# Banded attention with a two-layer FFN: the softmax division of units 16 to 47 moves from VectorE to ScalarE, and the hand-written order of all engines is written anew

## The chip, the cores and the metric

One core of one Trainium2 chip runs the kernel. The metric is device microseconds of one execution, lower is better. Engine names are those of the profile: PE is TensorE, DVE is VectorE, ACT is ScalarE, POOL is GpSimd, and SP is SyncE, which issues most of the DMAs.

## The reference

Four sequences of 768 tokens, eight heads of 64. Each token attends to 8 global tokens and to the last 96 tokens, with a bias that grows with distance. The softmax is divided by its row sum, and the result goes through a two-layer FFN (512 to 2048 to 512) with a leaky ReLU.

```python
scores = scale * np.matmul(q, k.transpose(0, 1, 3, 2)) + bias
scores = np.where(keep, scores, -1000000000.0)
scores = scores - np.max(scores, axis=-1, keepdims=True)
a = np.exp(scores)
a = a / (np.sum(a, axis=-1, keepdims=True) + 1e-09)
attn = np.matmul(a, v)
h = x @ w_in                      # x: 3072 x 512, w_in: 512 x 2048
g = np.maximum(0.01 * h, h)
out = g @ w_out                   # w_out: 2048 x 512
```

## The kernel before

**Work and stages.** The 3072 tokens are 24 steps of 128 tokens, and each step is two *units* of four heads, 48 units in all. Attention runs unit by unit and feeds the FFN. The FFN works on chunks of 3, 3, 2 and then four times 4 steps. The first three chunks are multiplied in the plain way, 16 hidden blocks each (48 blocks, words `F0` to `F47` and `H0` to `H47`); from the fourth chunk on each pair of blocks is made from seven smaller products (`Q`), which need sums of weight blocks and of activations. Every factor is kept as a high and a low part, so that each product is three matmuls.

**Who sets the order.** A table `ORDER` of 2574 words is walked by `fast_path` from first to last. Each word issues the instructions of one small step, and nearly all are pinned to that order on their own engine. Engines wait for one another through semaphores, but each runs its own instructions strictly in the table's order: an instruction that waits holds up everything behind it on its engine. The same is true of the DMA issues on SP and on POOL.

**The words.** For unit n: `Lq Lk Lv` load (SP); `S` scores (PE, L319); `B` adds the bias and takes the row maximum (DVE, L336); `E` exponentials and row sums (ACT, L352); `N` adds a small constant and inverts the sum (DVE, L377 and L378). Up to unit 15 the division lies in a small diagonal matrix (`G`, POOL) by which PE transposes (`T`). From unit 16 (`BY_DVE`) on, `M` divides, one instruction for each of four heads (DVE, L389, in `divide`); `D` transposes on DVE (L394) and sends the tile to DRAM (SP, L363); `I` fetches it back, turned, in four DMAs (SP, L369). `V` multiplies by the values (PE, L473) and `Xh` copies the result out (ACT, L483). `M` has parts `.0` to `.3`, as `B` and `E` have.

For FFN block n: `F` makes the hidden block (PE, L1051 to L1053); `ga` copies it out (ACT, L1063), `gb` applies the leaky ReLU (DVE, L1065), `gc` rounds the high part (ACT, L1067), `gd` makes the low part (DVE, L1069); `H` multiplies by the second weights (PE, L1087 to L1089). `H` needs `gc` for its first matmul and `gd` for its third. `c0` to `c31` convert the weights at the start.

For the later chunks: `C` makes sums of weight blocks for eight pairs (POOL L675, with four rounding steps each on ACT, L678); the sums of the first six pairs are built in one scratch area, stored to DRAM by `b` (SP, L726), and loaded back into weight memory that is no longer needed by `e` (POOL's DMA queue, L732; two loads for each pair, 768 KB for part `.0` and 256 KB for part `.1`). A pair's sums can only be started when the store of the pair before has left the scratch area. `A`, `Y`, `z` make sums and high and low parts of the activations (POOL L736, ACT L739, DVE or POOL L742). Then `Q` (PE, L711), `d y r h l` (adding up, ReLU, high and low part: DVE L756 L760 L766, ACT L750 L763), `J` (PE, L774) and `R` (weights from DRAM, POOL's queue, L722).

```python
for word in ORDER.split():
    step(word)
```

In `step`, `M` calls `divide(n, part)`, `D` calls `turned(n)`, which calls `move`, and `I` calls `fetch(n)`; `late` holds `C b e A Y z Q d r h l J R`.

Of the kernel before, what the change touches and what calls it, by code (L numbers as in the profile page):

```python
# [11 lines left out]
F32 = mybir.dt.float32  # L12
# [34 lines left out]
T7 g1c c8b F2 K7 k7 c9a N8 Lw11 c8c g1d V7 G8 g2a c9b S9 Lv10 Xh7 Xl7 T8 Lq6 H1 B9 Lk12 c9c Lw12 K8 k8 g2b E9 c8d V8
c9d S10 Lv11 g2c N9 Xh8 F3 g2d G9 Lk13 c10a B10 c11a Xl8 E10 c10b T9 H2 g3a N10 K9 Lw13 g3b k9 G10 c10c c11b g3c V9
T10 Lv12 Xh9 c10d Lw14 c11c Xl9 S11 K10 g3d F4 c12a B11 Lq7 k10 Lk14 E11 c11d H3 c12b g4a c13a N11 Lw15 c12c g4b V10
G11 c13b g4c F5 Lv13 Xh10 Xl10 g4d Lw16 c13c c12d T11 g5a S12 c13d c14a H4 K11 g5b Lk15 k11 B12 g5c E12 g5d V11 c14b  # L50
c15a S13 Lv14 Xh11 F6 Xl11 N12 Lw17 c14c c15b G12 H5 g6a B13 Lw18 c15c E13 g6b c15d F7 c14d g6c c17a g6d c16a N13 c17b
T12 g7a H6 K12 G13 k12 g7b Lw20 c17c c16b g7c F8 P6.0 P6.1 g7d Lw19 P6.2 c17d c16c T13 g8a c16d H7 g8b c18a g8c c18b
c19a F9 g8d Lw21 c18c c19b H8 g9a g9b Lw22 c19c c18d g9c F10 g9d c20a c19d c20b c21a H9 g10a g10b Lw23 c20c c21b g10c
F11 g10d Lw24 c21c V12 c20d g11a c21d H10 c22a Lv15 K13 g11b k13 c22b g11c c23a F12 g11d Lw25 c22c c23b S14 g12a H11
g12b Lw26 c23c B14 g12c E14 g12d F13 c22d c23d c24a N14 c25a H12 c24b G14 g13a g13b Lw27 c24c F14 c25b g13c T14 g13d
Lw28 c25c c24d g14a H13 g14b c26a c25d g14c g14d c27a F15 c26b H14 c27b Lw29 c26c g15a g15b Lw30 c27c F16 c26d g15c
g15d c28a c27d H15 c28b g16a c29a g16b Lw31 c28c F17 c29b g16c Lk16 O0 g16d c29c c28d g17a H16 O1 g17b c30a c29d g17c
O2 g17d c31a F18 c30b O3 O4 H17 c31b c30c g18a O5 g18b c31c C0.0 O6 F19 c30d g18c C0.1 g18d O7 c31d C0.2 H18 g19a O8
C0.4 C0.3 g19b C0.5 g19c O9 g19d F20 C0.6 Lk17 C0.8 C0.7 O10 C0.10 C0.9 H19 g20a O11 C0.11 g20b g20c O12 C0.13 C0.12
g20d F21 C0.14 O13 C0.15 Lq8 H20 C1.0 g21a O14 g21b C1.1 g21c O15 C1.2 g21d F22 C1.4 b0 C1.3 C1.5 H21 g22a C1.6 Xh12  # L60
g22b Xl12 g22c C1.7 g22d V13 C1.8 S15 Lv16 Xh13 K14 C1.10 F23 k14 Lq9 B15 C1.9 Xl13 Lk18 E15 Z2 H22 g23a N15 g23b g23c
V14 P22.0 g23d G15 S16 P22.1 Lv17 P22.2 F24 C1.11 Lk19 B16.0 Xh14 B16.1 E16.0 C1.13 B16.2 B16.3 E16.1 E16.2 Xl14 T15
E16.3 g24a N16 H23 C1.14 C1.12 M16.0 K15 M16.1 k15 C1.15 M16.2 M16.3 C2.0 V15 D16 b1 S17 C2.1 g24b Xh15 F25 C2.2 B17.0
g24c B17.1 E17.0 B17.2 Lk20 C2.4 E17.1 B17.3 C2.3 g24d E17.2 C2.8 S18 E17.3 I16 g25a H24 C2.5 N17 C2.9 g25b C2.6 Lk21
M17.0 g25c M17.1 C2.10 Lq10 C2.7 F26 M17.2 Lv18 M17.3 C2.11 g25d C2.13 B18.0 C2.12 B18.1 H25 E18.0 B18.2 C2.14 E18.1
B18.3 E18.2 D17 C2.15 E18.3 g26a N18 V16 Xl15 g26b I17 F27 Xh16 M18.0 g26c M18.1 M18.2 M18.3 Lv19 g26d S19 b2 g27a D18
H26 g27b B19.0 g27c B19.1 E19.0 F28 g27d E19.1 Lq11 B19.2 B19.3 I18 E19.2 E19.3 V17 C3.0 g28a N19 S20 g28b Lk22 Xh17
C3.1 H27 Lv20 M19.0 g28c C3.2 B20.0 Lk23 B20.1 E20.0 B20.2 C3.4 E20.1 B20.3 E20.2 g28d F29 E20.3 C3.8 M19.1 C3.3 N20
# [96 lines left out]
def fast_path(ctx, tc, qp, kp, vp, wi, wo, nvec, weights, wiboth, woboth, nmall, out, B, H, S):  # L165
# [999 lines left out]
```

## Time and profile before

| | |
|---|---|
| median of 3 runs | 662.97 us (662.08 to 663.45) |
| the profiled execution | 663.38 us, of which the span from first to last instruction is 661.6 us |
| PE busy | 622.5 us (94% of the span), granted clock 0.992 of full |
| DVE busy | 490.9 us (74%) |
| ACT busy | 279.9 us (42%) |
| POOL busy | 197.7 us (30%) |
| DMA | 130.64 MB, 197 GB/s on average |

PE is in use for nearly the whole span, so what the time can still lose is what PE stands idle, and what it runs at less than full clock. The share of PE is an average over stages: the first units and weight conversions, the plain chunks, and from about 300 us on a long even stretch of `Q` and `J`. A view by stage says where PE stands idle, and the view of waits says for whom.

### The profile page before, as it was taken

The numbers are of one execution on the slowest core, as the hardware profiler recorded it, in microseconds if no ns is written. First come the engines' busy times: TensorE is split into PE (matmuls) and PEld (weight loads), VectorE is DVE, ScalarE is ACT, GpSimd is POOL, SyncE is SP. The second block draws the span as 40 slices with busy tenths as digits, with TensorE's granted clock in tenths as the row PEclk, the third lists the DMA queues.
The fourth block names the chain that finished last, engine by engine and source line by source line (L and its number), as shares of the span: only waits on it lengthen the run. The fifth ranks groups of instructions, "written<-read, shape, count | busy, mean of one in ns | idle before, by whom it ended". The sixth has DMA issues, their size and how long they took to land.

```text
span 661.6 us, 16121 instructions
## 1 busy us (share of the span) xinstructions
PE 622.5 (94%) x6188; PEld 534.9 (81%) x6188; DVE 490.9 (74%) x1277; ACT 279.9 (42%) x801; POOL 197.7 (30%) x277
## 2 busy tenths in 40 slices
PE   5589999999999987889999999999999999999996
PEld 4478888898778865778888888888888888889894
DVE  7999999965867668497777976777987846655543
ACT  5978767546644353442224333234433223211111
POOL 3433401168553378280003400014300015200000
PEclk9999999999999999799999999999999999999998
DMA  8866645794767869656667497677686542433331
GB/s 292 288 223 203 212 138 174 279 418 139 226 218 246 286 203 311 180 171 193 192 200 223 129 283 223 169 209 231 181 257 187 160 144 68 160 114 107 96 96 69
DMA packets 64197, 130.64 MB, mean 197 GB/s; under 512 B 9072, under 2 KB 27504, under 8 KB 63344
## 3 DMA queue, kind: packets, MB, share of 16 engines
q1 hardware_dynamic: 53744, 91.78, 43.0%
q0 software_dynamic: 10368, 37.75, 19.1%
q8 instruction: 51, 0.84, 0.6%
q14 instruction: 34, 0.28, 0.2%
HBM read 96.47 MB, written 33.03 MB: 196 GB/s over the span
## 4 chain that ended last, share of the span: by engine, by line
PE 72%; DMA 10%; DVE 8%; ACT 4%; issue 2%; SPq 2%; POOL 1%; DVEq 0%; ACTq 0%; POOLq 0%
PE ps_q L711 13%; PE ps_two L774 12%; PE ps_o L774 12%; PE ps_o L711 9%; DMA room<-via 4%; PE ps_av L473 4%; DMA via<-pr 3%; PE ps_av L319 3%; PE ps_h L1051 3%; PE ps_h L1053 3%; PE ps_h L1052 3%; PE ps_o L1087 3%; PE ps_o L1089 3%; PE ps_o L1088 2%; ACT pr L352 2%
## 5 line engine op out<-in xcount | busy, mean ns | idle before, releaser
L763 ACT CAST rounded<-room 128x512 fp32r<-128x512 f32 x64 | 39.7, 620 | 194.4 <-DVE room L760 188.3
L722 POOL DMA_DIRECT2D wo<-w x60 | 32.2, 536 | 272.6 <-PE ps_two L774 257.9
L774 PE MATMUL ps_two<-wo,rounded 128*128 128x512 f32 x320 | 95.2, 395 | 0.0
L774 PE MATMUL ps_o<-wo,rounded 128*128 128x512 f32 x320 | 94.8, 394 | 0.0
L352 ACT ACTIVATE pr<-pr,nmall 128x192 f32<-128x192 f32 (+1 forms) x192 | 83.9, 440 | 17.6 <-DVE nmall L336 17.2
L756 DVE TENSOR_TENSOR room<-ps_o,room 128x256 f32<-128x256 f32 x128 | 54.1, 423 | 39.2 <-PE ps_o L711 29.0
L756 DVE TENSOR_TENSOR room<-ps_q,room 128x256 f32<-128x256 f32 x96 | 40.1, 418 | 34.0 <-PE ps_q L711 33.4
L1051 PE MATMUL ps_h<-rounded,wi 128*128 128x384 f32 (+1 forms) x192 | 62.6, 326 | 1.2 <-ACT atz L1063 1.1
L1052 PE MATMUL ps_h<-rounded,wi 128*128 128x384 f32 (+1 forms) x192 | 61.0, 318 | 0.6 <-POOL rounded L497 0.6
L1053 PE MATMUL ps_h<-rounded,wi 128*128 128x384 f32 (+1 forms) x192 | 60.9, 317 | 0.0
L774 PEld LDWEIGHTS ps_two<-wo,rounded 128*128 128x128 f32 x320 | 54.0, 188 | 6.1
L711 PEld LDWEIGHTS ps_o<-rounded,wo 128*128 128x128 f32 x384 | 53.9, 188 | 5.9 <-DVE pr L394 0.3
L774 PEld LDWEIGHTS ps_o<-wo,rounded 128*128 128x128 f32 x320 | 53.6, 188 | 5.8
L336 DVE CUSTOM_DVE_ANT_0 pr<-ps_av,nbw 128x192 f32<-128x192 f32 x140 | 42.3, 352 | 19.1 <-ACT room L483 14.1
L711 PE MATMUL ps_o<-rounded,wo 128*128 128x256 f32 x384 | 56.1, 282 | 0.0
L711 PE MATMUL ps_q<-rounded,wi 128*128 128x256 f32 x384 | 55.3, 280 | 0.4 <-ACT room L750 0.4
L711 PEld LDWEIGHTS ps_q<-rounded,wi 128*128 128x128 f32 x384 | 51.8, 189 | 3.8 <-ACT room L750 0.7
L760 DVE SCALAR_TENSOR_TENSOR room<-room 128x512 f32<-128x512 f32 x64 | 48.1, 753 | 1.7
L473 PEld LDWEIGHTS ps_av<-room,vr 64*64 64x64 f32 x1472 | 31.4, 134 | 21.8 <-issue 11.4
L675 POOL TENSOR_TENSOR room<-room 128x256 f32<-128x256 f32 (+1 forms) x56 | 45.4, 821 | 8.2 <-ACT room L678 5.8
L473 PE MATMUL ps_av<-room,vr 64*64 64x64 f32 (+1 forms) x1472 | 37.8, 239 | 8.1 <-DMA room<-via 6.7
L389 DVE TENSOR_SCALAR pr<-pr,rs 128x192 f32<-128x192 f32 (+1 forms) x128 | 43.8, 381 | 0.6
(131 smaller groups left out, 1322.8 us busy)
## 6 DMA issues: line engine op xcount, KB each, us to landing
wo<-w POOLq DMA_DIRECT2D x60, 512.0 KB, 3.8
via<-pr SPq DMA_DIRECT2D x28, 384.0 KB, 3.9
room<-via SPq DMA_DIRECT2D x112, 96.0 KB, 4.1
kr<-in_kp_dram SPq DMA_DIRECT2D x40, 256.0 KB, 4.6
vr<-in_vp_dram SPq DMA_DIRECT2D x40, 256.0 KB, 3.8
room<-in_wo_dram SPq DMA_DIRECT2D x16, 512.0 KB, 4.7
room<-in_wi_dram SPq DMA_DIRECT2D x16, 512.0 KB, 4.4
w<-wo SPq DMA_DIRECT2D x16, 512.0 KB, 8.2
```

The lines of the kernel that those rows point to most:

```text
L336: pin(nc.vector.tensor_tensor_reduce(out=head(u, pr, a, j), in0=own(u, ps[:, j, a * KW:(a + 1) * KW]), in1=nb, scale=-0.125, scalar=3.0e38 ...
L352: pin(nc.scalar.activation(out=p, in_=p, func=AF.Exp, scale=-1.0, bias=nm[:, 2 * a + j:2 * a + j + 1], accum_out=sm[:, 2 * a + j:2 * a + j ...
L389: pin(nc.vector.tensor_scalar(out=p, in0=p, scalar1=rs[:, n:n + 1], scalar2=1.0, op0=ALU.mult, op1=ALU.mult))
L473: tc.keep_in_program_order(nc.tensor.matmul(av[out, a, cols], lhsT=v[rows, t, j, :], rhs=near(rows, j, t, f), start=n == 0, stop=n + 1 == ...
L675: pin(nc.gpsimd.tensor_tensor(out=out, in0=a, in1=b, op=op))
L711: tc.keep_in_program_order(nc.tensor.matmul(out, lhsT=lhs[:, k], rhs=rhs[:, k], start=k == 0 and m == 0, stop=k == 1 and m == 2))
L756: pin(nc.vector.tensor_tensor(out=quarter[i][o], in0=lps[b][:, h * HB:(h + 1) * HB], in1=quarter[a][q], op=ALU.add))
L760: pin(nc.vector.scalar_tensor_tensor(out=t, in0=t, scalar=0.01, in1=t, op0=ALU.mult, op1=ALU.max))
L774: tc.keep_in_program_order(nc.tensor.matmul(o, lhsT=lhs, rhs=rhs, start=f == 0 and m == 0, stop=f == NF - 1 and m == 2))
L1051: tc.keep_in_program_order(nc.tensor.matmul(ps, lhsT=wh, rhs=xh[:, k, :CT], start=(k == 0), stop=False))
L1052: tc.keep_in_program_order(nc.tensor.matmul(ps, lhsT=wh, rhs=xl[:, k, :CT], start=False, stop=False))
L1053: tc.keep_in_program_order(nc.tensor.matmul(ps, lhsT=wl, rhs=xh[:, k, :CT], start=False, stop=(k == NK - 1)))
```

## The change

Two edits. In `divide` the multiplication by the inverse row sum is an activation (copy with a scale for each partition) on ACT in place of a tensor-scalar on DVE, for all units from 16 on (32 units, four instructions each). And `ORDER` holds the same 2574 words in another order.

```diff
@@ ORDER (2574 words, the same ones in another order) @@
-k2 K2 G3 Lw5 B4 Xh1 c2c V2 Xl1 E4 c3b S6 Lv5 T3 Lk9 Xh2 N4 K3 Lw6 Xl2 k3 c3c B5 V3 E5 G4 c3d Lv6 T4 c2d Xh3 K4 Xl3 k4
+N3 Xh1 k2 Lw5 K2 G3 B4 c2c V2 Xl1 E4 T3 Lv5 c3b S6 Lk9 Xh2 K3 Xl2 N4 Lw6 c3c k3 B5 V3 G4 E5 Lv6 c3d T4 c2d Xh3 K4 Xl3
...
@@ divide @@
                 p, n = head(u, pr, a, j), 2 * a + j
-                pin(nc.vector.tensor_scalar(out=p, in0=p, scalar1=rs[:, n:n + 1], scalar2=1.0, op0=ALU.mult,
-                                            op1=ALU.mult))
+                pin(nc.scalar.activation(out=p, in_=p, func=AF.Copy, scale=rs[:, n:n + 1]))
```

The edit in `divide` is one line shorter, so a line number of 390 or more in the kernel before is one less in the changed kernel. On PE the words from `Q1.1` to the end stand in the same order as before; only ahead of that PE's order differs too, by single words that changed places.

Three places show what moved. The first is POOL, from the loads of the kept weight sums (L732, `wo<-cw` is part `.0`, `wi<-cw` part `.1`) of pair 0 on. Before:

```order
L732 DMA wo<-cw 128x1536 x2
L732 DMA wi<-cw 128x512 x2
L732 DMA wo<-cw 128x1536
L736 TENSOR_TENSOR room<-room 128x512 x4
L742 TENSOR_TENSOR rounded<-room,rounded 128x512 x2
L732 DMA wo<-cw 128x1536 x2
L732 DMA wi<-cw 128x512
L732 DMA wo<-cw 128x1536
```

In the changed kernel, from its first load on:

```order
L731 DMA wo<-cw 128x1536
L731 DMA wi<-cw 128x512
L735 TENSOR_TENSOR room<-room 128x512 x4
L731 DMA wo<-cw 128x1536
L741 TENSOR_TENSOR rounded<-room,rounded 128x512 x2
L731 DMA wi<-cw 128x512
L731 DMA wo<-cw 128x1536
L731 DMA wi<-cw 128x512
L674 TENSOR_TENSOR room<-wi 128x256 x2
L674 TENSOR_TENSOR room<-room 128x256
L674 TENSOR_TENSOR room<-wi 128x256
L731 DMA wo<-cw 128x1536
```

Before, nine loads stood in two groups (and three, of part `.1`, further ahead); now all twelve come pair by pair, six ahead of the first `C6` (L674 here), and the other six among the sums of pairs 6 and 7, beside `Q0` to `Q2`.

The second place is SP around the moves (L363) and fetches (L369) of units 24 and 25, the two units whose tiles are 128x512. Before:

```order
L293 DMA kr<-in_kp_dram 128x512
L726 DMA cw<-room 128x2048
L363 DMA via<-pr 128x512 x2
L305 DMA vr<-in_vp_dram 128x512
L369 DMA room<-via 32x4x128 x8
L363 DMA via<-pr 128x768
```

In the changed kernel:

```order
L725 DMA cw<-room 128x2048
L363 DMA via<-pr 128x512
L305 DMA vr<-in_vp_dram 128x256
L369 DMA room<-via 32x4x128 x4
L363 DMA via<-pr 128x512
L293 DMA kr<-in_kp_dram 128x512
L287 DMA qs<-in_qp_dram 128x512
L369 DMA room<-via 32x4x128 x4
```

Before, both moves went ahead of both fetches, and the table had the fetch of unit 25 (`I25`) ahead of that of unit 24 (`I24`); now `I24` stands ahead of the move of unit 25.

The third place is DVE and ACT around FFN block 29 (`g29`: L1065 and L1069 on DVE, L1063 and L1067 on ACT before). Before, on DVE:

```order
L377 TENSOR_SCALAR rs<-sm 128x4
L378 RECIPROCAL rs<-rs 128x4
L389 TENSOR_SCALAR pr<-pr,rs 128x2x96 x4
L394 STREAM_TRANSPOSE pr<-pr 128x768
L1065 SCALAR_TENSOR_TENSOR atz<-atz 128x384
L389 TENSOR_SCALAR pr<-pr,rs 128x2x96 x2
L394 STREAM_TRANSPOSE pr<-pr 128x768
L1069 TENSOR_TENSOR rounded<-atz,rounded 128x384
```

In the changed kernel, on DVE:

```order
L377 TENSOR_SCALAR rs<-sm 128x4
L378 RECIPROCAL rs<-rs 128x4
L1064 SCALAR_TENSOR_TENSOR atz<-atz 128x384
L393 STREAM_TRANSPOSE pr<-pr 128x768
L1068 TENSOR_TENSOR rounded<-atz,rounded 128x384
```

And on ACT in the changed kernel, at the same block:

```order
L352 ACTIVATE pr,sm<-pr,nmall 128x2x96 x4
L1062 COPY atz<-ps_h 128x384
L389 ACTIVATE pr<-pr,rs 128x2x96 x4
L1066 CAST rounded<-atz 128x384
L677 CAST room<-room 128x256
L1062 COPY atz<-ps_h 128x384
```

Between `N20` and `g29d` DVE had six divisions and two transposes, and now has one transpose; the four divisions of unit 20 stand on ACT between the copy and the cast of block 29.

## Rows read from the trace of the kernel before

**Rows 1.** Busy us by stage: PE, PEld, DVE, ACT, POOL; granted clock, DMA share, GB/s.
```profile
0.00:41.00 41.00, 24.61 (x618) 20.32 (x619) 35.52 (x136) 29.33 (x100) 17.90 (x37) 1.00 0.83 281
41.00:160.00 119.00, 118.83 (x1241) 102.50 (x1240) 103.64 (x232) 80.19 (x203) 42.17 (x64) 1.00 0.65 224
160.00:300.00 140.00, 125.02 (x1257) 103.99 (x1256) 103.81 (x278) 65.30 (x215) 76.20 (x98) 0.98 0.72 226
300.00:600.00 300.00, 298.89 (x2747) 259.41 (x2746) 218.85 (x579) 96.26 (x271) 57.19 (x71) 1.00 0.62 185
```
**Rows 2.** Waits of PE, 160 to 300 us: us in total, times, longest.
```profile
PE ps_av L473 <- DMA room<-via: 6.2, 4, 4.7
PE ps_two L1087 <- ACT rounded L1067: 2.2, 1, 2.2
PE ps_two L1089 <- DVE rounded L1069: 2.2, 3, 1.6
PE ps_o L1089 <- DVE rounded L1069: 2.0, 2, 1.6
PE ps_av L473 <- issue: 1.4, 1, 1.4
```
**Rows 3.** Chain that ended last: start, us, what, 247 to 268 us.
```profile
247.56 6.59 DMA via<-pr
...
258.22 9.11 DMA room<-via
```
**Rows 4.** Timeline of POOL, its DMA issues from 241 to 261 us.
```profile
241.25 1.10 POOL L732 DMA_DIRECT2D wo<-cw  x2
242.34 1.07 POOL L732 DMA_DIRECT2D wi<-cw  x2
244.69 0.56 POOL L732 DMA_DIRECT2D wo<-cw  x1 [1.28 <-PE ps_two L1089]
...
256.75 1.10 POOL L732 DMA_DIRECT2D wo<-cw  x2
257.84 0.54 POOL L732 DMA_DIRECT2D wi<-cw  x1
260.12 0.53 POOL L732 DMA_DIRECT2D wo<-cw  x1 [1.75 <-PE ps_two L1089]
```
**Rows 5.** DMA issues over the span: count, KB each, median us to landing.
```profile
via<-pr SPq DMA_DIRECT2D x28, 384.0 KB, 3.9
room<-via SPq DMA_DIRECT2D x112, 96.0 KB, 4.1
```
**Rows 6.** Busy us by stage, the stretch after PE's longest wait.
```profile
267.40:272.00 4.60, 4.53 (x36) 3.48 (x37) 1.53 (x9) 1.22 (x4) 0.00 (x0) 0.50 0.41 138
```
**Rows 7.** Timeline of DVE around block 29, 191 to 198 us.
```profile
191.27 1.95 DVE L389 TENSOR_SCALAR pr<-pr,rs 128x192 f32<-128x192 f32 x4
...
194.98 1.50 DVE L389 TENSOR_SCALAR pr<-pr,rs 128x192 f32<-128x192 f32 x2
...
197.42 0.52 DVE L1069 TENSOR_TENSOR rounded<-atz,rounded 128x384 fp32r<-128x384 f32 x1
```
**Rows 8.** Timeline of POOL and of ACT ahead of block 38, 231 to 235 us.
```profile
231.99 1.42 POOL L675 TENSOR_TENSOR room<-wi 128x256 f32<-128x256 f32 x2 [5.44 <-DMA cw<-room]
...
234.25 0.40 ACT L678 CAST room<-room 128x256 fp32r<-128x256 f32 x1 [4.59 <-POOL room L675]
234.56 0.40 ACT L1067 CAST rounded<-atz 128x256 fp32r<-128x256 f32 x1
```
**Rows 9.** Groups by line and shape, 160 to 300 us (last row: 300 to 600).
```profile
L389 DVE TENSOR_SCALAR pr<-pr,rs 128x192 f32<-128x192 f32 x44 | 19.3, 480 | 0.1
...
L352 ACT ACTIVATE pr<-pr,nmall 128x192 f32<-128x192 f32 x48 | 21.4, 448 | 8.4 <-DVE nmall L336 8.3
L483 ACT COPY room<-ps_av 128x256 f32<-128x256 f32 x11 | 4.1, 373 | 15.9 <-PE ps_av L319 12.8 <-PE ps_av L473 3.1
...
L389 DVE TENSOR_SCALAR pr<-pr,rs 128x192 f32<-128x192 f32 x68 | 19.4, 326 | 0.4
```

More of the change, by code (lines that the diff above doesn't have):

```diff
@@ L47 @@
[L47 to L56, printed above, removed]
@@ new lines @@
+l11.1 Q12.1 Lq21 B39.0 J11.00 B39.1 E39.0 B39.2 y12.1 B39.3 Q12.6 E39.1 Q12.2 I38 E39.2 d12a E39.3 J11.01 d12b N39
+Q12.5 Lk42 M39.0 J11.02 d12c M39.1 M39.2 Q12.3 M39.3 J11.03 D39 Q12.7 R13.0 d12d J11.10 r12.0 J11.11 d12e h12.0 d12f
+Q12.4 l12.0 J11.12 d12g J11.13 r12.1 V37 R13.1 h12.1 S40 Lv40 Xh37 l12.1 Q13.1 I39 B40.0 J12.00 B40.1 y13.1 B40.2
+E40.0 Q13.6 B40.3 E40.1 Q13.2 E40.2 d13a E40.3 J12.01 d13b Lk43 N40 Q13.5 M40.0 J12.02 d13c M40.1 M40.2 Q13.3 M40.3
+J12.03 D40 Q13.7 R14.0 d13d J12.10 r13.0 J12.11 d13e h13.0 d13f Q13.4 l13.0 J12.12 d13g J12.13 r13.1 V38 R14.1 h13.1
@@ new lines @@
+S41 l13.1 Xh38 Q14.1 A5.1 B41.0 B41.1 E41.0 J13.00 I40 B41.2 y14.1 B41.3 Q14.6 E41.1 E41.2 Q14.2 d14a E41.3 Lv41
+J13.01 N41 Lq22 Q14.5 d14b M41.0 Lk44 M41.1 J13.02 M41.2 d14c M41.3 Q14.3 D41 J13.03 d14d Q14.7 R15.0 r14.0 J13.10
+d14e h14.0 J13.11 d14f l14.0 Q14.4 J13.12 d14g r14.1 J13.13 V39 h14.1 R15.1 S42 l14.1 Xh39 Q15.1 A5.2 B42.0 B42.1
+E42.0 J14.00 Lk45 B42.2 y15.1 B42.3 I41 Q15.6 Y5.0 A5.3 E42.1 Q15.2 z5.0 Y5.5 J14.01 A5.4 Y5.2 Lv42 E42.2 d15a E42.3
+z5.2p d15b Q15.5 z5.5 J14.02 Y5.4 Q15.3 J14.03 Y5.3 d15c d15d Q15.7 R16.0 r15.0 J14.10 Y5.1 d15e J14.11 d15f h15.0
@@ new lines @@
+l26.0 Q26.4 J25.12 d26g r26.1 J25.13 Q27.1 h26.1 R27.1 J26.00 y27.1 l26.1 Q27.6 Q27.2 d27a J26.01 d27b Q27.5 J26.02
+d27c Q27.3 J26.03 d27d r27.0 Q27.7 R28.0 J26.10 h27.0 d27e d27f J26.11 l27.0 Q27.4 J26.12 d27g r27.1 J26.13 Q28.1
+h27.1 R28.1 J27.00 y28.1 l27.1 Q28.6 Q28.2 d28a J27.01 d28b Q28.5 J27.02 d28c Q28.3 J27.03 d28d r28.0 Q28.7 R29.0
+J27.10 h28.0 d28e d28f J27.11 l28.0 Q28.4 J27.12 d28g r28.1 J27.13 Q29.1 h28.1 R29.1 J28.00 y29.1 l28.1 Q29.6 Q29.2
+d29a J28.01 d29b Q29.5 J28.02 d29c Q29.3 J28.03 d29d r29.0 Q29.7 R30.0 J28.10 h29.0 d29e d29f J28.11 l29.0 Q29.4
@@ L157 @@
+J28.12 d29g r29.1 J28.13 Q30.1 h29.1 R30.1 J29.00 y30.1 l29.1 Q30.6 Q30.2 d30a J29.01 d30b Q30.5 J29.02 d30c Q30.3
+J29.03 d30d r30.0 Q30.7 R31.0 J29.10 h30.0 d30e d30f J29.11 l30.0 Q30.4 J29.12 d30g r30.1 J29.13 Q31.1 h30.1 R31.1
+J30.00 y31.1 l30.1 Q31.6 Q31.2 d31a J30.01 d31b Q31.5 J30.02 d31c Q31.3 J30.03 d31d r31.0 Q31.7 J30.10 h31.0 d31e d31f
+J30.11 l31.0 Q31.4 J30.12 d31g r31.1 J30.13 X3 h31.1 J31.00 l31.1 J31.01 J31.02 J31.03 J31.10 J31.11 U6.0 J31.12 U6.1v
+J31.13 U6.2 U6.3v
 """
```

192 lines of the change are left out of this document (91 added, 101 removed).

## The prediction, made before the changed kernel ran

> **What bounds the kernel now.** I read the busy time by stage first, because a share over the whole span mixes stages. PE is busy 298.89 of the 300 us from 300 to 600, and 118.83 of 119 from 41 to 160 [rows 1]. There the time is PE's own work, and no other engine can give anything. PE stands idle in two places: 16.4 us in the first 41 us (41.00 less 24.61), and 15.0 us between 160 and 300 us (140.00 less 125.02) [rows 1]. The first stage has no instruction `M`, since units below 16 do not use it. So the second one is where this change can pay, and its 15.0 us are the first bound of the gain.
>
> The waits of PE in that stage say for whom it stood [rows 2]. The largest is `V` waiting for a fetch of the turned tile: 6.2 us in four waits, the longest 4.7. Then one wait of 2.2 us for ACT's cast (`gc` ahead of `H`), five waits of 4.2 us together for DVE's low part (`gd` ahead of the third matmul of `H`), the longest of each kind 1.6, and one of 1.4 us with no releaser in the profile. I followed the largest back along the chain: the move of a tile to DRAM took 6.59 us and the last fetch DMA 9.11 us [rows 3], against medians of 3.9 and 4.1 for the same two transfers over the span [rows 5]. What else was on the DMA engines then? POOL's timeline shows it: nine of the twelve loads of weight sums were issued in two bursts, five from 241.25 on and four from 256.75 to 260.12 [rows 4], that is 2.8 MB just ahead of the slow move and 2.6 MB around the slow fetch. Behind the longest wait the granted clock is 0.50 for 4.6 us, with PE busy 4.53 of them [rows 6]: PE runs at the lower of its two levels, 1.2 GHz, after having stood. That work at full clock would take half, so the wait cost another 2.3 us that no idle time shows.
>
> The profiled execution took 663.4 us (its span is 661.6), 0.4 above the median of 662.97; the sum below starts from 663.4.
>
> **The loads.** The twelve loads are the same in size and number, so nothing is removed; they are spread over a longer stretch, pair by pair, and the fetch of unit 24 no longer stands on SP behind the move and fetch of unit 25. By the order there are now four FFN blocks and more of PE's work between that fetch and its `V`, and in between only one or two loads at a time. With the move at 3.9 and the fetch at 4.1 in place of 6.59 and 9.11 [rows 3, 5] it would land 7.7 us sooner, more than the 6.2 us that all four waits make up. I take the whole 6.2 [rows 2] as gone, and with them the clock's 2.3 [rows 6]. Bounds: 4.7 us at least, the longest wait alone; 8.5 at most. What the loads cost in their new place: six of them, 3 MB, now fall beside `Q0` to `Q2`. They hide behind fetches (unit 27 on) that have over 20 us of PE work ahead of their `V` there; without that lead the cost is one more fetch drawn out by 5.0 us (9.11 less 4.1) [rows 3, 5].
>
> **The parked cast.** At 234.25 us ACT rounds a weight sum after 4.59 us of waiting for POOL, which itself had waited 5.44 us for the store of the previous sums; the cast for block 38 stands behind it and runs at 234.56 [rows 8]. That is the 2.2 us wait for ACT [rows 2]. In the new order the store of pair 4 goes ahead by about one FFN block, and the first rounding step of pair 5 stands ahead of block 38's copy, with the whole of block 37's `H` and block 39's `F` behind it. I take the 2.2 as gone; the bounds are 0 and 2.2.
>
> **The multiplication, off DVE.** In this stage stand 13 units, 52 instructions. On DVE they took 480 ns on average, against 326 after 300 us [rows 9]; 52 by 0.48 is 25.0 us (the eight narrower ones counted like the others, so an upper value). This queue of divisions is one place where `gd` comes late: between 191.27 and 196.48 DVE runs six divisions, 3.45 us, and the low part of block 29 follows only at 197.42 [rows 7], while PE waits 1.6 us [rows 2]. With the six gone it comes at least 3.45 us sooner, so that wait goes. The other long wait, 1.6 us too, is at block 43, where DVE holds no division; there only the spreading of POOL's work beside it can help, and I take half. Of the 4.2 us I count 2.4 as gained; the bounds are 0 and 4.2.
>
> **The multiplication, on ACT.** The trace has no such instruction. The nearest rows are the exponential of the same 128x192 tile, 448 ns, which has two pointer operands and an accumulator, and the plain copy of 128x256 out of PSUM, 373 ns [rows 9]. I take 410, between them, since it has one pointer and the smaller tile. So 52 by 0.41 is 21.3 us on ACT in this stage (19.4 to 23.3), on top of 65.30 busy of 140 [rows 1]. The rule of the Trainium skill that speaks against this is in "ScalarE: Activation LUTs", Rules for kernel authors: multiplications belong on VectorE, not on ScalarE. By the figures of the same page (What ACT_TABLE_LOAD costs), 186 ns, 0.833 ns for each of 192 elements and 93 ns for a pointer operand, one costs an estimated 439 ns, and 22.8 us in the stage; the row of VectorE here is 480, so the rule does not hold by the length of one instruction in this stage, while after 300 us (326) it does.
>
> After 300 us there are 19 units, 76 instructions, 31 us more on ACT with 96.26 busy of 300 [rows 1]. PE's 298.89 hide all of it; without that cover it is worth 76 by 84 ns (410 less 326), 6.4 us. The gain that DVE has there, 76 by 326 ns, is hidden in the same way. I cost both at nothing.
>
> **What the new places add.** Now each `D` waits for ACT, and so do the move, the fetch and `V` behind it. What is queued behind `M` on ACT are `gc` casts for which PE waits. By the order, the four divisions of unit 20 stand between the copy and the cast of block 29: 1.6 us in a chain that had no division. The tightest fetch is that of unit 17: its last division stands on ACT behind the exponentials of unit 18, and the `V` comes about 7 us of PE work after its transpose, while move and fetch take 8.0 by the medians [rows 5]. I add 1 us for that, and 2 us for casts that come late. Bounds: nothing (the stage after 300 us loses 1.1 us in 300 under an order of the same kind [rows 1]), and 19.4 us, all 52 on PE's path at 373 ns [rows 9].
>
> **The first 160 us.** No instruction changes there, only single words change places (some of `T`, `K`, `c`, and unit 12 and 14 come earlier). I count 0; with 16.4 us idle in the first 41 us [rows 1], I allow 2 either way, an estimate of an eighth of it.
>
> **The sum.** 663.4 - 6.2 - 2.3 - 2.2 - 2.4 + 3.0 = **653.3 us**, a gain of about 10 us or 1.5%.
>
> **The rivals.** *Only the loads pay.* ACT is an ordered queue as DVE is, and what `gd` gains, `gc` loses: the 2.4 is not there, and the new waits are 5 in place of 3, so 657.7. For it: the divisions now stand between copies and casts of gate blocks. Against it: DVE had 103.81 busy of 140 and ACT 65.30 [rows 1], so the move is from the fuller to the emptier queue.
>
> *The spread loads move the wait.* Twelve loads are still 6 MB beside everything else, and DMA is at a share of 0.72 in the stage [rows 1]. If two fetches are drawn out by 5.0 us each, with one more drop of the clock (2.3), 653.3 becomes 665.6; with one, 658.3. Against it: before, only the bursts did harm, and each load now has compute instructions of POOL ahead of it. This is also how the change would fail to do what it says, if POOL runs late and the loads bunch up again.
>
> *Slower: ACT's queue ends last.* By the rule of the page named above this move would cost. As a mechanism here: if the four divisions of a unit stand ahead of a `gc` that PE awaits, that `H` is late by 4 by 373 ns, 1.5 us [rows 9]. Without the 2.4, the other gains are 10.7, so it decides from 8 of the 13 units on; with all 13, 663.4 - 10.7 + 19.4 = 672.1. For it: one parked cast already cost PE 2.2 us [rows 2, 8]. Against it: between an `F` and its `H` PE has another block's work, so that a delay of 1.5 us is not all seen.
>
> **How the numbers follow.** My forecast has 0.58, with 649.5 to 657 as its own range (the bounds of 2 for the first stage, and 0 to 6 for the new waits). Only the loads pay: 0.20, at 657.7. The wait moves: 0.12, half of it at 658 and half near no change. ACT ends last: 0.10. About 0.2%, 1.3 us, is what a measurement of this kernel can tell from no change. Faster than that: 0.58 + 0.20 + 0.06 = 0.84; the same 0.06; slower 0.10. The range goes from 647, where the new waits are nothing and the first stage gains 2 and block 43's wait goes too, to 661, which takes in the second case and the near half of the third.
>
> **What would show it.** PE's idle time between 160 and 300 us at 3 to 6 us in place of 15.0; no wait of `V` for a fetch over 2 us; no stretch at half clock inside the span; the loads 2 to 4 us apart and more; 128 instructions of the division on ACT at 370 to 450 ns. The multiplications are wrong as a gain if PE's waits for `gc` exceed 4 us; the loads are wrong if fetches still land after 7 us or more ahead of a waiting `V`. An idle time of PE in the first 41 us that differs from 16.4 by over 2 us would make the prediction wrong for a reason that I do not expect.

## The result, and the profile after

| | before | after |
|---|---|---|
| median of 4 runs each | 663.21 us | 652.82 us (652.63 to 655.13) |
| ratio of after to before | | 0.9849, 95% interval 0.9818 to 0.9880 |
| the profiled execution (its span) | 663.38 us (661.6) | 655.13 us (653.0) |
| span less PE busy | 661.6 - 622.5 = 39.1 us | 653.0 - 619.9 = 33.1 us |

The forecast was 653.3 us. Two later comparisons of the same two kernels gave 0.9921 (0.9870 to 0.9972) and 0.9895 (0.9855 to 0.9935), so that the three ratios put the gain at 0.8 to 1.5%, 5 to 10 us. The forecast gain of 10 us lies at the upper end of this, and its nearness to 652.82 is partly luck: the profiled execution itself took 655.13, 1.8 more than the sum that was made for it.

The busy time by stage of the changed kernel (columns as in [rows 1]), the lines that answer to those:

```profile
0.00:41.00 41.00, 24.14 (x615) 20.02 (x616) 34.96 (x133) 28.85 (x99) 17.77 (x37) 1.00 0.80 277
41.00:160.00 119.00, 118.47 (x1239) 102.31 (x1240) 104.08 (x235) 78.77 (x199) 41.33 (x60) 1.00 0.65 225
160.00:300.00 140.00, 133.57 (x1345) 113.75 (x1347) 87.44 (x240) 85.60 (x276) 81.05 (x103) 0.98 0.75 241
300.00:600.00 300.00, 297.58 (x2729) 258.70 (x2721) 200.77 (x497) 122.47 (x344) 57.55 (x72) 1.00 0.59 180
```

PE's idle time between 160 and 300 us fell from 15.0 to 6.4 us (140 less 133.57). The other stages lost a little: 0.5 us in the first, 0.4 in the second, 1.3 from 300 to 600 us. DVE has 16.4 us less to do in the stage, and ACT 20.3 more.

PE's waits from 160 to 300 us (columns as in [rows 2]):

```profile
PE ps_av L319 <- ACT room L482: 2.7, 1, 2.7
PE ps_two L1088 <- DVE rounded L1068: 2.5, 2, 2.0
PE ps_two L1086 <- ACT rounded L1066: 0.6, 1, 0.6
```

The two longest on PE's timeline (start, us, what, and the idle time before it with its releaser):

```profile
255.13 0.50 PE L1088 MATMUL ps_two<-wo,rounded 128*128 128x512 f32 x1 [2.01 <-DVE rounded L1068]
...
276.55 0.60 PE L319 MATMUL ps_av<-kr,qs 64*64 64x192 f32 x4 [2.73 <-ACT room L482]
```

No wait of `V` for a fetch is left; it was 6.2 us [rows 2]. The parked cast went from 2.2 to 0.6. The 2.0 us wait is new in its cause, and the 2.7 us wait is new altogether. Behind both, the granted clock is about half for 3.4 us, where before one such stretch stood [rows 6]:

```profile
255.50:258.90 3.40, 3.40 (x15) 3.15 (x14) 3.10 (x10) 1.81 (x7) 3.32 (x5) 0.52 1.13 402
276.00:279.40 3.40, 2.85 (x22) 2.17 (x23) 0.80 (x1) 1.59 (x6) 2.50 (x4) 0.52 0.74 231
```

**Where the new waits come from.** The first is on DVE. Its timeline, and POOL's beside it:

```profile
250.74 3.40 DVE L377 TENSOR_SCALAR rs<-sm 128x4 f32<-128x4 f32 x1
254.17 0.18 DVE L378 RECIPROCAL rs<-rs 128x4 f32<-128x4 f32 x1
254.27 0.81 DVE L1068 TENSOR_TENSOR rounded<-atz,rounded 128x256 fp32r<-128x256 f32 x1
```

```profile
246.10 4.43 POOL L735 TENSOR_TENSOR room<-room 128x512 f32<-128x512 f32 x3 [4.38 <-ACT room L482]
250.48 0.57 POOL L731 DMA_DIRECT2D wo<-cw  x1
251.07 2.51 POOL L741 TENSOR_TENSOR rounded<-room,rounded 128x512 fp32r<-128x512 f32 x2
253.51 0.57 POOL L731 DMA_DIRECT2D wi<-cw  x1
254.08 0.54 POOL L731 DMA_DIRECT2D wo<-cw  x1
254.60 0.55 POOL L731 DMA_DIRECT2D wi<-cw  x1
...
258.43 0.57 POOL L731 DMA_DIRECT2D wo<-cw  x1
```

`N26` adds a constant to four numbers of each partition. It held DVE for 3.40 us while POOL made its two low parts; the reciprocal of the same four numbers right behind it took 0.18. `g44d`, for which PE waits, stood behind it. The Trainium skill ("SBUF — State Buffer", Who interferes with whom) says that a tensor-scalar on VectorE can take the port pair that GpSimd uses, and that whoever comes second is blocked for the other's whole instruction, while ScalarE waits for nobody. In the trace the addition starts 0.33 us ahead of the two sums, while POOL issues the load before them, and ends 0.06 us after the issue of the load behind them (253.51 and 0.57). Experiments 8, 10 and 11 test that place.

The loads show that the plan did not hold: POOL waited 4.38 us for ACT ahead of its sums, and five loads then went out within 8 us, 2.8 MB (three of 768 KB and two of 256 KB). The second wait stands on SP and on ACT:

```profile
257.51 0.33 SPq L363 DMA_DIRECT2D via<-pr  x1
...
265.83 1.75 SPq L369 DMA_DIRECT2D room<-via  x4
...
268.15 0.38 SPq L529 DMA_DIRECT2D out_dram<-atz  x1
```

```profile
273.38 0.58 ACT L527 COPY atz<-ps_two 128x512 f32<-128x512 f32 x1 [4.12 <-DMA out_dram<-atz]
...
276.14 0.35 ACT L482 COPY room<-ps_av 128x256 f32<-128x256 f32 x1
```

SP's fetch of unit 26 could go only 8.3 us after its move was issued, where a move took 3.9 by the median before [rows 5]. The store of a plain output (`P47.0`) stands behind that fetch and the next move on SP: ACT's copy for it was done at 266.33, and it went 1.8 us later. It was then out for 5.2 us. The second copy into the same buffer (`P47.1`) waits on ACT for that store, and behind it stands ACT's copy of unit 26 (`Xh26`), which frees the bank that `S29` writes. That the bunched loads brought this about is argued and not shown: in one execution of experiment 7 the same loads are bunched as closely and the wait is absent.

### The profile page after: what moved, and what is told of

It is laid out like the page before. It is cut to its first block, busy times and chain, and to the rows that moved or that the text cites. A ratio compares the mean times of both kernels' runs of the same rounds, so it can differ in the third digit from the quotient of the medians.

```text
span 653.0 us, 16154 instructions
## 1 busy us (share of the span) xinstructions
PE 619.9 (95%) x6188; PEld 535.3 (82%) x6188; DVE 451.2 (69%) x1149; ACT 322.9 (49%) x929; POOL 200.9 (31%) x277
## 4 chain that ended last, share of the span: by engine, by line
PE 76%; DVE 8%; DMA 4%; POOL 4%; ACT 3%; issue 2%; SPq 0%; ACTq 0%; POOLq 0%; DVEq 0%
PE ps_two L773 13%; PE ps_q L710 13%; PE ps_o L773 13%; PE ps_o L710 10%; PE ps_av L472 4%; PE ps_av L319 4%; POOL room L674 4%; PE ps_h L1050 3%; PE ps_h L1052 3%; PE ps_h L1051 3%; PE ps_o L1086 3%; PE ps_o L1088 3%; PE ps_o L1087 3%; DMA cw<-room 2%; DMA via<-pr 2%
## 5 line engine op out<-in xcount | busy, mean ns | idle before, releaser
L352 ACT ACTIVATE pr<-pr,nmall 128x192 f32<-128x192 f32 (+1 forms) x192 | 83.8, 439 | 13.3 <-DVE nmall L336 13.1
L389 ACT ACTIVATE pr<-pr,rs 128x192 f32<-128x192 f32 (+1 forms) x128 | 48.4, 440 | 17.9 <-DVE rs L378 17.7
L674 POOL TENSOR_TENSOR room<-room 128x256 f32<-128x256 f32 (+1 forms) x56 | 45.6, 827 | 3.0 <-ACT room L677 0.5
L674 POOL TENSOR_TENSOR room<-wi 128x256 f32<-128x256 f32 x32 | 28.1, 888 | 49.9 <-DMA cw<-room 25.1
L1064 DVE SCALAR_TENSOR_TENSOR atz<-atz 128x384 f32<-128x384 f32 (+1 forms) x48 | 29.5, 615 | 19.0 <-ACT atz L1062 18.7
```

The lines of the kernel that those rows point to most:

```text
L352: pin(nc.scalar.activation(out=p, in_=p, func=AF.Exp, scale=-1.0, bias=nm[:, 2 * a + j:2 * a + j + 1], accum_out=sm[:, 2 * a + j:2 * a + j ...
L389: pin(nc.scalar.activation(out=p, in_=p, func=AF.Copy, scale=rs[:, n:n + 1]))
L674: pin(nc.gpsimd.tensor_tensor(out=out, in0=a, in1=b, op=op))
```

## The experiments

The kernels are named in the text by their numbers. Every ratio is to the kernel before, run beside them on the same chip: 1 to 4 in one comparison, 5, 8, 9 and the first of 7 in a second, 6, 10 and the second of 7 in a third, 11 in a fourth. Single runs of before ranged from 656.5 to 667.9 us there, so a difference of under 3 us between two kernels is not told apart. "Idle" is PE's idle time from 160 to 300 us in the profiled execution (before: 15.0).

| | order | division | loads | median us | ratio (95%) | idle us |
|---|---|---|---|---|---|---|
| 1 | new | DVE | spread | 660.24 | 0.9975 (0.9937 to 1.0012) | 9.2 |
| 2 | before | ACT | bursts | 660.48 | 0.9974 (0.9937 to 1.0011) | 10.0 |
| 3 | before | DVE | spread | 659.93 | 0.9949 (0.9918 to 0.9980) | 8.0 |
| 4 | new | ACT | bursts | 659.20 | 0.9934 (0.9901 to 0.9968) | 8.0 |
| 5 | before, `I24` first | DVE | bursts | 663.85 | 1.0042 (1.0000 to 1.0084) | 13.1 |
| 6 | before | ACT | spread | 660.67 | 0.9951 (0.9917 to 0.9985) | 8.5 |
| 7 | the change again | | | 655.08; 654.19 | 0.9921; 0.9895 | 7.7; 4.4 |
| 8 | the change without the addition | | | 655.24 | 0.9903 (0.9861 to 0.9945) | 6.3 |
| 9 | 8 and a later copy | | | 656.38 | 0.9909 (0.9869 to 0.9949) | 5.7 |
| 10 | the change, low parts on DVE, later copy | | | 660.46 | 0.9979 (0.9950 to 1.0007) | 6.9 |
| 11 | the change, two low parts on DVE | | | 658.18 | 0.9945 (0.9914 to 0.9976) | 6.9 |

### 1. The new order with the division on DVE

```diff
-                pin(nc.scalar.activation(out=p, in_=p, func=AF.Copy, scale=rs[:, n:n + 1]))
+                pin(nc.vector.tensor_scalar(out=p, in0=p, scalar1=rs[:, n:n + 1], scalar2=1.0, op0=ALU.mult,
+                                            op1=ALU.mult))
```

> The new order, with the division left on VectorE. My theory (the loads, the fetch of unit 24 and the parked cast carry 10.7 of the gain, the move to ScalarE 2.4 less new waits): 652 to 656 us; the waits of PE for the low parts from VectorE between 160 and 300 us rise from 3.0 to 4 to 7 us, no wait of V for a fetch over 2 us. Rival 1 (the engine carries the gain): 659 us or more, near the kernel before. Rival 2 (the engine is worth nothing, or costs): 650 to 653, since the waits for ScalarE go.

0.9975, 660.24 us: the theory's 652 to 656 failed, and the first rival's time is what was measured. With the division left on DVE, the new order is worth at most a little. PE's waits in the stage:

```profile
PE ps_two L1089 <- DVE rounded L1069: 2.9, 3, 2.2
PE ps_av L319 <- ACT room L483: 2.1, 1, 2.1
PE ps_o L711 <- DVE room L756: 1.4, 2, 0.9
PE ps_o L1089 <- DVE rounded L1069: 1.1, 1, 1.1
```

No wait of `V` for a fetch stands here either, but 5.4 us of waits for DVE in three of these rows, against 2.7 in the changed kernel. So in this order the division on ACT pays by what it takes off DVE. These rows account for 2.7 us of the 5 to 7 by which the medians lie above those of 7; the rest was not followed.

### 2. The order before with the division on ACT

The same edit the other way round, in the kernel before.

> The old order, with the division on ScalarE. My theory: the waits for the fetch of unit 24 (6.2 us and 2.3 of half clock) and for the parked cast (2.2) stay, the low part of block 29 is no longer late: 659 to 664 us. Rival 1 (the engine carries the gain): 655 or less. Rival 2 (ScalarE's queue becomes the one that is late): over 664.

0.9974, a time that the theory gave, but not by its waits. The 4.7 us wait of `V24` is gone although the loads stand in their old bursts. In its place the hidden matmul of block 45 waits 4.2 us for ACT's copy. POOL and ACT at that place:

```profile
253.18 5.70 POOL L735 TENSOR_TENSOR room<-room 128x512 f32<-128x512 f32 x4 [7.58 <-DMA cw<-room]
```

```profile
254.46 0.62 ACT L738 CAST rounded<-room 128x512 fp32r<-128x512 f32 x1 [6.84 <-POOL room L735]
254.99 0.37 ACT L1062 COPY atz<-ps_h 128x256 f32<-128x256 f32 x1
```

The store of pair 5's weight sums (`b5`), issued at 241.30, was out for 11.9 us; POOL's activation sums need that scratch area, ACT's cast of them waits, and the copy for block 45 is parked behind it. In the kernel before the same store came in 6.6 us, and the tile of unit 24 was the late one. The same group of five loads is beside both transfers, and which of the two is drawn out decides who waits. POOL, which had waited, issued the second group only from 261.93 on, when the fetch of unit 24 had nearly landed (256.75 before [rows 4]).

### 3. The order before with the loads spread

The twelve words `e` go where the change has them, and nothing else moves.

```diff
-e0.1 ... e1.1 ... e2.1 ... e0.0 ... e1.0 e3.1 e4.1 e2.0 ... e3.0 e4.0 e5.1 e5.0
+e0.0 ... e0.1 ... e1.0 ... e1.1 e2.0 ... e2.1 ... e3.0 ... e3.1 ... e4.0 ... e4.1 ... e5.0 ... e5.1
```

> The old order and the division on VectorE, with only the twelve loads of the weight sums put behind the PE words at which the new order has them. My theory (bursts draw out the move and the fetch): PE's waits for the fetched tile fall from 6.2 to under 2 us, no half clock around 267 us, 654.5 to 659 us. Rival (the fetch of unit 24 is late because it stands behind the move and fetch of unit 25 on SyncE's queue, whatever the loads do): 661 to 664, with a wait of 3 us or more still at that V.

0.9949, 659.93 us, just above the theory's range, but with its waits: the idle time falls to 8.0 us, so the loads alone remove most of what goes. `V`'s wait for the fetch is gone, and so is the wait for the parked cast, without the division on ACT:

```profile
PE ps_two L1089 <- DVE rounded L1069: 2.4, 3, 1.9
PE ps_q L711 <- DVE room L756: 2.0, 2, 1.2
...
PE ps_two L1087 <- ACT rounded L1067: 0.7, 2, 0.4
```

Three early loads of part `.1` stood between 218 and 226 us before; without them the store that POOL waits for [rows 8] lands 5.7 us after its issue in place of 7.9. Four of the loads stand within 2.2 us here too, from 255.51 on, behind the fetch of unit 24; what is gone is the group of five beside its move.

### 4. The changed kernel with the loads in the old bursts

The edit of 3 the other way round.

> The changed kernel with only the twelve loads put back behind the PE words at which the old order had them, in two bursts. My theory (loads in bursts cost what they did): 656 to 661 us, with a V that waits 3 us or more for its fetch. Rival (the place of the fetch on SyncE's queue is what counts, and the new order has that): 652 to 654.5.

0.9934, 659.20 us: a time in the theory's range without the wait that it named. The parked cast is back, 3.2 us in two waits, and no fetch makes `V` wait over 0.4:

```profile
PE ps_two L1086 <- ACT rounded L1066: 3.2, 2, 1.9
PE ps_av L319 <- ACT room L482: 2.8, 1, 2.8
...
PE ps_av L472 <- DMA room<-via: 0.4, 1, 0.4
```

So the wait for unit 24 can be taken away by the loads alone (3) or by the rest of the change (here), and the parked cast hangs on the loads. The two gains overlap, and adding them counts one wait twice.

### 5. Only the fetch of unit 24 first

```diff
-H41 Xh23 A3.1 D25 ... z3.5 g43a A3.3 Y3.5 g43b I24 F44
+H41 Xh23 A3.1 I24 D25 ... z3.5 g43a A3.3 Y3.5 g43b F44
```

> The old order, the division on VectorE and the loads in bursts, with one word moved: the fetch of unit 24 goes on SyncE's queue ahead of the move of unit 25. Theory after the first four runs (two causes stand behind the longest wait, and taking away either one ends it): PE's wait of 4.7 us for the fetch of unit 24 falls under 1 us and the half clock behind it goes: a ratio of 0.987 to 0.992. Rival (the bursts alone decide, the fetch would be drawn out in any place): the wait stays over 3 us, 0.997 or more.

A miss: 1.0042, no gain. `V24` no longer waits, and the same 4.9 us stand at block 45 (ACT, and POOL ahead of it):

```profile
259.06 5.71 POOL L736 TENSOR_TENSOR room<-room 128x512 f32<-128x512 f32 x4 [8.35 <-DMA cw<-room]
```

```profile
260.35 0.62 ACT L739 CAST rounded<-room 128x512 fp32r<-128x512 f32 x1 [7.61 <-POOL room L736]
260.88 0.36 ACT L1063 COPY atz<-ps_h 128x256 f32<-128x256 f32 x1
```

The store of pair 5 went at 246.38 and was out for 12.7 us. These are the waits of experiment 2 without any change of engine. The place on SP's queue by itself gains nothing; that the loads cost, experiment 3 shows.

### 6. Both parts in the order before

Experiments 2 and 3 together: does the rest of the new order matter?

> The order before, with only the twelve loads in their new places and the division on ScalarE. Theory 1 (the two named parts are the gain, and they act on different waits: the bunch of loads draws out either the tile of unit 24 or the store of pair 5's weight sums, whichever is issued beside it, and the division holds VectorE): the time is that of the changed kernel within 0.3%, ratio to before 0.984 to 0.992, idle time of TensorE from 160 to 300 us 5.5 to 7.5 us, no wait of V for a fetch over 1 us, the wait of the hidden matmul behind VectorE's and ScalarE's late activation sums (4.15 us with the old bursts and the division on ScalarE) gone or below 1 us. Theory 2 (the order had to be planned anew, since divisions on ScalarE in the old places hold up casts): ratio 0.994 to 0.999, at least one wait for ScalarE's cast or copy over 2 us.

0.9951, a median of 660.67 against 654.19 of the changed kernel beside it (five of the twelve runs lie within the changed kernel's 652.4 to 657.9, seven above; the means are 659.1 and 654.5, 4.7 apart with a standard error of 1.2). Theory 2's ratio holds, though its single wait of over 2 us does not: the loss is spread. From 160 to 300 us the idle time is 8.5, against 4.4 of the changed kernel in the same comparison, and waits for a fetch stand after 300 us. PE's waits from 160 to 300 us:

```profile
PE ps_h L1050 <- ACT atz L1062: 2.4, 2, 1.3
PE ps_two L1088 <- DVE rounded L1068: 2.1, 2, 1.9
```

And from 300 to 600 us:

```profile
PE ps_av L472 <- DMA room<-via: 2.6, 2, 1.8
```

In the old places the divisions leave ACT's copies for `F` late; the changed kernel has 0.2 us there, and experiment 3, with the division on DVE, 0.4. What delays the fetch at 390 us was not followed.

### 7. The changed kernel twice more

> The changed kernel as it is, on the same chip as the three others. Both theories: a ratio to the kernel before of 0.985 again, within 0.003. If its ratio is nearer to 0.993 than to 0.985, the gap to the four runs before this one was the chip and not the parts.

> The changed kernel once more, on the chip of this comparison: ratio to before 0.985 to 0.993, with both waits of its first profile (about 2 us at 256 us for VectorE's low part, 2.7 to 3.6 us at 277 us for ScalarE's copy of unit 26).

The first of these expectations failed: 0.9921 is not within 0.003 of 0.985, and lies nearer to 0.993. By what was set down beforehand, the gap between 0.985 and experiments 1 to 4 was then the chip and not the parts. The two later ratios hardly tell the changed kernel from experiments 3 and 4; experiment 1 lies above both, with an interval that overlaps that of the first only; and beside experiments 6 and 10, on one chip, the changed kernel is the faster.

Counting the first, the wait of block 44 stood in all three profiles (2.0, 2.1 and 2.0 us). The wait for unit 26's copy did not: 2.7 us in the first profile, 3.6 in the second, and none in the third, whose expectation of 2.7 to 3.6 failed. There the store of `P47.0` was issued at 268.60 and the second copy waited 1.07 us where it had waited 4.12:

```profile
271.75 0.59 ACT L527 COPY atz<-ps_two 128x512 f32<-128x512 f32 x1 [1.07 <-DMA out_dram<-atz]
```

The same store, from the same place in the order, is out for 3.2 us in one execution and 5.2 in another. The five loads are bunched as closely in all three profiles (251.90 to 259.88 in the third), so the bunch alone does not make this wait, and why the store differs is open.

### 8. The changed kernel without the addition

`N` inverts the sum directly; the addition of 1e-9 is left out, here and in 9.

```diff
-        pin(nc.vector.tensor_scalar(out=rs, in0=sm, scalar1=1e-9, scalar2=None, op0=ALU.add))
-        pin(nc.vector.reciprocal(out=rs, in_=rs))
+        pin(nc.vector.reciprocal(out=rs, in_=sm))
```

> The changed kernel without the addition of 1e-9 to the row sums (the 48 tensor-scalar instructions of 128x4; each row sum is at least 1 here, so that the addition of 1e-9 in fp32 changes no bit of it). Theory: the one of unit 26 took 3.40 us beside GpSimd's work, against 0.18 elsewhere, and held up the low part of block 44 behind it; without it PE's wait of 2.0 us there goes: 1.5 to 3.5 us less than the changed kernel. Rival (VectorE stands as long for the next instruction beside GpSimd, the reciprocal): the same time within 0.7 us.

0.9903, 655.24 us against 655.08 of the changed kernel beside it: the time of the rival. The reciprocal, now first, is over in 0.17 us ahead of POOL's two low parts (from 250.53). The low part of block 44 behind it falls beside them and takes the place of the addition, and PE's longest wait for DVE there is 1.3 us in place of 2.1:

```profile
250.20 0.17 DVE L377 RECIPROCAL rs<-sm 128x4 f32<-128x4 f32 x1
250.99 2.87 DVE L1067 TENSOR_TENSOR rounded<-atz,rounded 128x256 fp32r<-128x256 f32 x1 [0.62 <-ACT rounded L1065]
```

### 9. Also the second plain copy behind the copy of unit 26

```diff
-... Q0.7 P47.1 C6.10 B28.0 ... r0.1 Xh26 Q1.1 ...
+... Q0.7 C6.10 B28.0 ... r0.1 Xh26 P47.1 Q1.1 ...
```

> The same without the addition, and the copy of the last plain result (second tile) on ScalarE behind the exponentials of unit 28 and the copy of unit 26, not ahead of them. Theory: that copy waited 4.12 us for the store of the first tile, which uses the same buffer, and the copy of unit 26, for which the scores of unit 29 wait, stood behind it; now PE's wait of 2.7 us there goes, with the half clock behind it: 2.5 to 4.5 us less than without the addition alone. Rival (the scores of unit 29 wait for something else that is as late): within 1 us of it.

0.9909, where 2.5 to 4.5 us less than 8 were expected. The wait for `Xh26` is gone; 2.9 us at `Q1` for DVE stand in its place. Now the low part of the hidden block (`l0.1`), whose tile lies in the memory of that output buffer, waits for the later store:

```profile
274.70 1.02 DVE L764 TENSOR_TENSOR btz<-room,rounded 128x512 fp32r<-128x512 f32 x1 [4.19 <-DMA out_dram<-atz]
```

### 10. All low parts of POOL on DVE, and the later copy (addition kept)

```diff
-z3.1p z3.6p z4.2p z4.1p z4.6p z5.2p z5.1p z5.6p z6.2p z6.1p z6.6p
+z3.1  z3.6  z4.2  z4.1  z4.6  z5.2  z5.1  z5.6  z6.2  z6.1  z6.6
```

> The changed kernel with the eleven low parts of activation sums that GpSimd makes given to VectorE, and the second copy of plain block 47 put behind the copy of unit 26. Theory: the late low part of block 44 (3.40 us of VectorE for a 128x4 instruction) and the wait at 355 us come from VectorE and GpSimd working at once: both go, 2.0 and 1.8 us, with the half clock behind them, and the wait for unit 26's copy, 2.7; in exchange 11 instructions of 0.45 to 0.95 us on VectorE. Ratio to before 0.978 to 0.986, idle from 160 to 300 us 2.5 to 4.5 us. Rival: GpSimd's three sums (4.4 us) beside them hold VectorE just the same, and the wait stays over 1 us: ratio as the changed kernel's.

0.9979, 660.46 us against 654.19 of the changed kernel beside it: slower, and the expected gain failed. The theory of the 3.40 us holds, since the addition takes 0.85 with POOL's pair gone; block 44 waits 0.6. Here and in 11 the addition ends within 0.01 us of the end of POOL's second load issue, so the issues may hold DVE as well; no run tests them alone. But `l0.1` now waits 5.38 us for the store, and PE 4.2 us behind it, and the wait at 355 us (2.4 us here) stays: beside POOL's three activation sums there a low part on DVE takes 1.71 us, and 0.69 behind them. The addition and `l0.1`:

```profile
252.25 0.85 DVE L377 TENSOR_SCALAR rs<-sm 128x4 f32<-128x4 f32 x1
...
278.70 1.72 DVE L765 TENSOR_TENSOR btz<-room,rounded 128x512 fp32r<-128x512 f32 x1 [5.38 <-DMA out_dram<-atz]
```

### 11. Only two low parts on DVE

Only `z3.1p` and `z3.6p` change; the copy stays where the change has it.

> The changed kernel with only the two low parts of activation sums of the third kept chunk (z3.1, z3.6) on VectorE in place of GpSimd; the copy of block 47 stays where the change has it. Theory: the 128x4 addition takes under 1.5 us in place of 3.40, the third matmul of block 44 waits under 1 us in place of 2.0, and since the copy is not moved, no wait of 4 us for the buffer's store follows beside Q1; ratio to before 0.983 to 0.989, a gain on the changed kernel of 2 to 4 us at most, which this comparison may just not tell. Rival: the two extra instructions hold VectorE as long as the lock did, and the wait only moves to the next block: idle of TensorE from 160 to 300 us as in the changed kernel, 4.4 to 6.4 us, ratio 0.988 to 0.993.

0.9945: below both ranges' gain. The addition takes 0.84 us and block 44 waits 0.6, as the theory has it, but a wait of `V26` for its fetch is back, in PE's waits of the stage:

```profile
PE ps_av L472 <- DMA room<-via: 2.3, 1, 2.3
```

POOL's timeline at its first loads there:

```profile
250.77 0.57 POOL L731 DMA_DIRECT2D wo<-cw  x1
251.34 0.54 POOL L731 DMA_DIRECT2D wi<-cw  x1
251.86 0.55 POOL L731 DMA_DIRECT2D wo<-cw  x1
252.38 0.56 POOL L731 DMA_DIRECT2D wi<-cw  x1
...
256.57 0.57 POOL L731 DMA_DIRECT2D wo<-cw  x1
```

POOL's two low parts (2.5 us) had stood between the first load and the next three. Without them four loads go out within 2 us, and the move of unit 26, issued at 256.93, lands so late that its fetch goes only at 266.24. That is only 0.4 us later than in the changed kernel and does not make a wait of 2.3; experiment 10 has the same four loads within 2.2 us, and its move took 8.2 us, as the changed kernel's 8.3. The fetch itself took up to 4.8 us to land here, and at most 2.5 in the changed kernel and in 10. And PE, which had lost less time at block 44, came to `V25` at 265.55 and not at 267.61. What drew the fetch out is open; a load was issued beside it at 266.39, which the changed kernel has at 268.46.

None of the repairs beats the changed kernel, though 9, 10 and 11 took away a wait that they named; 8 only shortened one.

## Why the prediction was right, and where it was wrong

- **The stage.** Right: the gain lies between 160 and 300 us. Idle 3 to 6 us was forecast there, and 6.4, 7.7 and 4.4 were measured, two of the three above it.
- **The fetch, -6.2.** Right in the changed kernel: no wait of `V` is left. The reason was half the story. The 6.59 us of [rows 3] are the move of unit 25; that of unit 24, issued at 243.77, took 9.1. I let it fall to the median of 3.9, but in the changed kernel it took 7.8, 7.8 and 7.9 us, in its three profiles. What changed is that it was issued 8 us earlier, and that its fetch landed in 2.0 to 3.0 us in place of 9.11. On SP (changed kernel):

```profile
235.74 0.33 SPq L363 DMA_DIRECT2D via<-pr  x1
...
243.57 2.80 SPq L369 DMA_DIRECT2D room<-via  x4
```

The store `b5` is drawn out beside the bursts as well as the tile, and the fetch order that I counted on gives nothing by itself (experiment 5). That the wait is gone in experiments 3 and 4 alike shows that either part of the change is enough for it; in 2 and 5 a wait of like length took its place.
- **The half clock, -2.3.** Wrong for the profiled execution: two shorter stretches stand in place of one. PE was busy 3.40 + 2.85 us in them, which cost half, 3.1 us, where 2.3 was to go. The step that failed is "no stretch at half clock inside the span".
- **The parked cast, -2.2.** Right in size (0.6 is left), wrong in its cause. I put it down to the new order of the store and the rounding steps; the loads alone do it (experiment 3), and the new order without them does not (experiment 4).
- **The low parts, -2.4.** 4.2 became 2.5, so -1.7. The wait that I gave to the queue of divisions (block 29) is gone. A late block stays with 2.0 us, now block 44 in place of 43: POOL's sums were replanned, but POOL ran late, and an addition of DVE fell beside two of its instructions.
- **New waits, +3.0.** Right in size, 3.1 (2.7 and twice 0.2), wrong in place. I named unit 17's fetch and casts behind divisions; neither shows over 0.6. It came from the store of a plain output, issued 1.8 us late on SP and then out for 5.2.
- **Beside the sum.** The 1.4 us wait with no releaser is gone, for which I had counted nothing; from 300 to 600 us PE is idle 2.4 us in place of 1.1, 1.8 of it at 355 us, where DVE's low parts run beside POOL; the first 160 us lose 0.8 more. Over the whole span idle time fell by 6.0 us and PE's busy time by 2.6, of which I can name no cause. That it stands about where the 2.3 of half clock were to go, which did not go, is luck.
- **The division's price.** I took 410 ns; the trace shows 447 for the 128x192 tile:

```profile
L389 ACT ACTIVATE pr<-pr,rs 128x192 f32<-128x192 f32 x112 | 43.0, 447 | 17.3 <-DVE rs L378 17.2
```

The page "ScalarE: Activation LUTs" of the Trainium skill (What ACT_TABLE_LOAD costs) gave an estimate of 439 for this tile, and the trace lies 2% above it. The rule of the same page of the Trainium skill (Rules for kernel authors) that multiplications belong on VectorE would have made the change a loss. Experiment 1 against the changed kernel (0.9975 against 0.985 to 0.992, though not beside one another) speaks for the opposite here. On DVE the 56 divisions of the stage in experiment 1 took 273 to 1326 ns (median 318), on ACT in the changed kernel 386 to 468 (median 444). So ACT is mostly the slower engine for one, but for the 128x192 tile the means are 524 on DVE and 449 on ACT: DVE's long ones stand beside POOL's instructions.

- **The rivals.** "Only the loads pay" gave 657.7 for a kernel whose division brings nothing; experiment 3, which has no division on ACT, lies at 659.93. "The spread loads move the wait" happened in part, by the way named: POOL ran late and the loads bunched up again, five in 8 us. That happened in all three profiles; a wait for unit 26's copy (2.7 and 3.6 us) with half clock behind it stood in two of them, so that the loads are its cause is not shown. "ACT's queue ends last" did not happen in the new order (0.6 us for casts), though in the old one ACT's copies cost 2.4 us (experiment 6).
- **What the sum could not see.** The parts do not add. Spread loads alone are at 0.9949, the division alone at 0.9974, both in the old order at 0.9951, the new order with the division on DVE at 0.9975, all together at 0.985 to 0.992. The rows of waits show why: each part alone takes away the same wait of `V24`, or puts another in its place. Experiment 6, beside the changed kernel, says that the rest of the new order is worth something. How much, the intervals don't settle: it lies 6.5 us above the changed kernel by the medians, 4.7 by the means and 3.7 by the ratios, whose intervals overlap.
- **The spread.** My own range of 649.5 to 657 does not follow from the bounds named for it: 653.3 less 3 and 2 is 648.3, and with 3 and 2 more 658.3. The 0.2% that a measurement was to tell was too small; the intervals here reach 0.3 to 0.5% to either side.

## What to carry to other kernels

When a transfer is late, list all that is under way beside it and who waits for each: taking the one wait away that ends last gives the next one its place, here 4.9 us for 4.7. On queues in a fixed order, as here, an engine change and the order have to be made together, and a term that is taken from one wait can be claimed by two edits. A local repair has to be costed with what it sets free: a buffer kept longer, or an engine that comes earlier to its next transfer.

## What was not expected of the hardware

- An addition over 128x4 elements on DVE took 3.4 us, in all three profiles of the changed kernel, beside two POOL instructions of together 2.51 us; without them 0.85. The section of the Trainium skill named above has the rule, and the trace agrees with it in that POOL's work blocks DVE. What of that work does it is not settled: in five profiles (three of the changed kernel, 10 and 11) the addition ends within 0.06 us of the end of a load issue on POOL. It is not an affair of tensor-scalars alone: with that instruction left out, a 128x256 tensor-tensor took 2.87 us in its place.
- A wait of the same length is followed by half clock in one execution and not in another: the 1.8 us at 355 us had a granted clock of 1.00 behind it in the first profile of the changed kernel, and of 0.53 in the second. In the second and third profile PE also ran at about half clock for some 3 us around 36 us (0.53 and 0.51), and not in the first. Each such stretch costs PE about half its length, so two executions of one kernel differ by 2 us and more with nothing changed in its code.
